# A larger ring of exp tiles, paid for by the ring of DVE tiles, with new assumed delays in a planned kernel

## The chip, the cores and the metric

One core of one Trainium2 chip. The metric is the device time of one launch in microseconds. Ratios are the mean time of one kernel's fast runs over the mean of the other's fast runs of the same rounds, so not quite the ratio of the medians that are quoted.

## The reference

Two independent branches on sequences of 2048 rows and 640 columns, side by side in the output: a diagonal state-space model, and attention with 32 heads of 20 columns over one shared key and value head.

```python
h = Lam_bar * h + Bu[t]                        # for each t
y = 2.0 * einsum("blp,dp->bld", hseq, Cmat).real + x * Dskip
...
scores = einsum("bhqd,bkd->bhqk", q, k) * (Dh ** -0.5)
p = softmax(scores, axis=-1)
o = einsum("bhqk,bkd->bhqd", p, v)             # then @ wo
return concatenate([a, b], axis=-1)
```

The attention decides the time: 32 heads of 2048 x 2048 scores are 2048 tiles of 128 x 512, and each element needs an exponential.

## The kernel before: the parts that matter

Before anything is built, Python plans the whole run: a discrete-event planner with assumed durations and assumed delays from engine to engine picks, for each engine, what it does next. Only the order that comes out is emitted, with the waits that the data need. The planner is run with 24 seeds, and the plan that it thinks ends first is taken.

```python
class Schedule:
    OUT = {"pe": 200.0, "act": 130.0, "dve": 110.0, "pool": 150.0, "dma": 60.0}   # end -> seen elsewhere, ns
...
    def planned(self):
        for seed in range(self.PLANS):            # 24
            ...                                   # keep the plan with the smallest end
```

ACT takes score tiles by two or three in one exp instruction. A *fill* is the PE step that writes the scores of the next exp (and perhaps a tile for DVE) into one of two three-bank slots:

```python
    def fill(self, op, i):
        n = min(self.cap[i], NTILE - self.tile_n)
        if n == 3 and self.want_own():
            own = self.take_d(used)               # third bank: a tile for DVE
        if own is not None:
            n = 2                                 # then ACT's exp has two tiles
        ...
        h = self.pr_take(n)                       # n slots of the exp ring (NPT = 24)
```

DVE tiles get an integer approximation of exp: one first step (reads PSUM), then three shifted copies made by DVE or POOL, so that one tile uses four slots of a second ring. It has `NDS = 20` slots, and `MORE = 21` further ones once the memory of the transposed input, the query weights and the query tiles is free (10, 6 and 5 slots; the change leaves it the first 10). A tile goes to DVE only if slots are free:

```python
    def want_own(self):
        ...
        return len(self.d_free()) > len(self.SHIFTS) - 1       # 4 shifts

    def can_d(self):
        ...
        if b > self.pv_b and len(self.d_free()) < len(self.SHIFTS) + self.due_copies():
            return False                          # a tile of the next block needs more free slots
```

*Fillers* are matmuls without use, meant to keep TensorE's clock up: before the attention and at its start (`warm_source`), and later, 256 columns wide, wherever the planner counts fewer than `KEEP = 3500` columns in 3 us (`keep_source`).

Of the kernel before, what the change touches and what calls it, by code (L numbers as in the profile page):

```python
# [42 lines left out]
class Schedule:  # L43
# [3 lines left out]


    ENGINES = ("pe", "act", "dve", "pool", "sp")
    OUT = {"pe": 200.0, "act": 130.0, "dve": 110.0, "pool": 150.0, "dma": 60.0}  # L50
    OWN = {"pe": 0.0, "act": 60.0, "dve": 115.0, "pool": 100.0}
    URGENT = 1.0

# [74 lines left out]
    def begin(self, op, eng):  # L128
        if op.hook is not None:
            op.hook(op)  # L130
        op.start = self.t
        if op.late:
            self.late_from = self.t + op.dur + self.PAUSE
        if eng == "pe":
            if op.mode != self.mode:
                op.dur += self.SWITCH
                self.mode = op.mode
            self.loads.append((self.t, op.load))
        if op.port:
            if eng == "pool" and self.port_last["dve"] is not None:  # L140
                op.after.append(self.port_last["dve"])
            self.port_free[eng] = self.t + op.dur + (self.LOCK if eng == "pool" else 0.0)
            self.port_last[eng] = op
            self.at(self.port_free[eng])
        if op.dma_key is not None:
            self.free[eng] = self.t + op.tail * len(op.fns)
            s = max(self.t + 1300.0, self.dma_free.get(eng, 0.0), self.pipe)
            self.dma_free[eng] = self.pipe = s + op.dur
            op.end = max(s + op.dur + 700.0, self.free[eng] + 1700.0) + op.land
        else:  # L150
            if op.table is not None and op.table != self.table:
                self.table = op.table
                op.dur += self.TABLE
            op.end = self.t + op.dur + op.tail
            self.free[eng] = self.t + op.dur - (self.EARLIER.get(eng, 0.0) if op.psum else 0.0)
        self.order.append(op)
        self.at(self.free[eng])
        for lag in (0.0, 60.0, 100.0, 110.0, 115.0, 130.0, 150.0, 200.0):
            self.at(op.end + lag)

    stay = staticmethod(lambda: True)
# [253 lines left out]
class Build:  # L415
# [3 lines left out]
    NOP = 7  # L419
    NRD = 3  # L420
    NDS = 20
    MORE = 21
    SHARE = 0.265

    SHIFTS = ((0, 0.2421875), (32, 0.201171875), (64, 0.169921875), (96, 0.142578125))
# [13 lines left out]
    def build(self):  # L439
        nc = self.nc  # L440
        with ExitStack() as o:
            self.banks = []
            self.slots = []
            sizes = list(self.CHUNKS) + [1] * (8 - sum(self.CHUNKS))
            self.psum = [o.enter_context(nc.psum_tensor(f"{'SC' if i < len(self.CHUNKS) else 'MB'}{i}", [128, 512 * n], FP32))
                         for i, n in enumerate(sizes)]
            self.alloc(o)
            base = nc.sbuf_bytes_remaining
            with ExitStack() as p1:
                self.alloc_early(p1)  # L450
                early = base - nc.sbuf_bytes_remaining
            with ExitStack() as p2:
                self.alloc_late(p2)
                late = base - nc.sbuf_bytes_remaining
                if late < early:
                    self.sb(p2, "pad", [128, (early - late) // 4 + 8], FP32)
                plan = self.planned()
                shares = {k: self.EARLY for k in self.LATE}
                shares.update({k: self.EARLY for k in ("pb0", "pb1", "lb", "qt")})
                shares.update({f"W{c}_0": self.EARLY + ["pb0", "pb1"] for c in range(NC)})  # L460
                shares.update({f"W{c}_1": self.EARLY + ["lb", "qt", "pc0", "pc1"] for c in range(NC)})
                shares.update({"pc0": ["lb"], "pc1": ["qt"]})
                shares.update({f"CB{c}": [f"xbT{i}_{k}" for i in range(2) for k in range(NC)] for c in range(NC)})
                shares.update({f"CT{tb}_{c}": [f"xn{tb}"] for tb in range(2) for c in range(NC)})
                shares.update({f"DR{self.NDS + i}": over for i, over in enumerate(self.dr_over)})
                shares["WOt"] = [f"BT{i}_{c}" for i in range(2) for c in range(NC)]
                shares.update({f"OPT{k}": [f"BA{i}_{c}" for i in range(2) for c in range(NC)] for k in self.EARLY_O})
                em = Emitter(nc, plan.s.order, [b.key for b in plan.banks], shares)
                em.plan()
                with nc.Block() as block:  # L470
                    em.emit(block)
# [36 lines left out]
    def alloc(self, o):  # L508
# [9 lines left out]
        for c in range(NC):  # L518
            for m in range(2):
                self.dr_at.append(2048 * c + 640 + 512 * m)  # L520
                self.dr_over.append([f"xbT{i}_{c}" for i in (1, 2, 3)])
        for m in range(6):
            self.dr_at.append(ends[0] + 512 * m)
            self.dr_over.append(["wqa", "wqb"])
        for m in range(NC):
            self.dr_at.append(ends[1] + 512 * m)
            self.dr_over.append([f"QP{m}"])
        self.xaT = sb(o, "xaT", [128, NC, 2, 512], BF16)
        self.BT = sb(o, "BT", [128, 2, NC, 640], BF16)
        self.BA = sb(o, "BA", [128, 2, NC, 640], BF16)  # L530
# [124 lines left out]
    def program(self):  # L655
        self.lay_banks()
        self.firsts, self.row_mm, self.stage_dma, self.buf_user, self.unit_due = [], {}, {}, {}, {}
        self.tile_n = 0
        self.rem = [[collections.deque(range(NKC)) for _ in range(4)] for _ in range(NQB * NGG)]
        self.act_b = 0  # L660
        self.free_banks = list(self.banks)
        self.vp_op, self.kt_op, self.vs_op = {}, {}, {}
        self.tasks = []
        self.evac_op, self.norm_op, self.part_op = {}, {}, {}
        self.q_op, self.qd_op, self.half_op, self.scat_op, self.rd_op, self.brow_op = {}, {}, {}, {}, {}, {}
        self.o_ops, self.y_ops, self.w_op, self.xa_op = {}, {}, {}, {}
        self.state_op = {}
        self.owner = [None] * self.NPT
        self.pr_at = 0
        self.waiting = []  # L670
        self.dhold = [Holder(i) for i in range(self.NDS)]
        self.d_open = []
        self.d_left = collections.defaultdict(int)
        self.d_count = 0
        self.d_per = collections.defaultdict(int)
        self.pvq = {b: [[], [], [], []] for b in range(NQB * NGG)}
        self.pv_filled = {b: 0 for b in range(NQB * NGG)}
        self.pv_b = 0
        self.pv_first = {}
        self.outs = 0  # L680
        self.s.stay = lambda: self.started
        self.constants()
        self.loads()
        self.kv_steps()
        self.ssm_scalars()
        self.background()
        self.s.spawn(self.attention())
        self.s.spawn(self.manager())
        self.s.spawn(self.late_loads())
        self.s.spawn(self.more())  # L690
        self.free_banks.remove(self.pvbank)
        self.s.sources["pe"].append(self.pv_source)
        self.s.sources["pe"].append(self.warm_source)
        self.s.sources["pe"].append(self.d_source)
        self.s.sources["pe"].append(self.keep_source)
        self.s.sources["dve"].append(self.copy_source)
        self.s.sources["act"].append(self.act_source)
        self.s.sources["pool"].append(self.pool_source)

    def warm_source(self):  # L700
# [3 lines left out]
        p = self  # L704
        if self.started:
            if self.s.recent(3000.0) > self.WARM:
# [1 line left out]
            fns = self.four(self.pvbank, [p.VZ[:]] * 4, p.KT[:, 0:512], True, True)  # L708
            return Op("pe", fns, self.mmt(512), prio=3.5, mode="C", load=512.0, reads=["VZ", "KT0"], writes=[self.pvbank.key],
                      deps=[self.c_op["VZ"], self.kt_op[0]])  # L710
        return Op("pe", [self.mm(self.pvbank.ap, p.PR[:, 0, 0:128], p.PR[:, 0, :], True, True)], 260.0, prio=9,
                  load=512.0, deps=[self.zero_op], reads=["PR0"], writes=[self.pvbank.key], hook=self.warm_last)

    WARM = 4500.0
    V_AT, BOUND_AT = (-88, -87), -99

# [467 lines left out]
    def fill(self, op, i):  # L1184
# [16 lines left out]
        ents = []  # L1201
        for x, m in enumerate(tiles):
            b, kc, j = self.score(op, m, t[:, 512 * x:512 * x + 512], banks[x])
            ents.append((b, kc, j, p.PR[:, h.index + x, :]))
        first = [] if own is None else [self.fill_d(op, own, banks[2])]
        if first:
            other = self.slot_last[1 - i][0]
# [6 lines left out]
        op.reads = sorted(set(op.reads))  # L1214
        op.dur = self.mmt(512, len(op.fns))
        op.load = 128.0 * len(op.fns)
        dst = p.PR[:, h.index:h.index + n, :]
        ex = self.act(lambda e: e.activation(dst, t[:, 0:512 * n], ACT.Exp, scale=1.0 / UNIT),  # L1218
                      0.8333 * 512 * n + 64, table="exp",
                      deps=[op], reads=[b.key for b in banks[:n]], writes=keys, prio=0.5,  # L1220
# [32 lines left out]
        return h  # L1253

    def pr_next(self, n):
        return self.pr_at if self.pr_at + n <= self.NPT else 0

    def tight(self):

# [171 lines left out]
    def more(self):  # L1431

        yield lambda: NQB - 1 in self.row_mm and self.s.done([self.row_mm[NQB - 1]]) \
            and all(self.s.done([self.qd_op[NQB - 1, i]]) for i in range(NC))
        self.dhold += [Holder(self.NDS + i) for i in range(self.MORE)]

    def d_free(self):

# [865 lines left out]
```

## Time and profile before

| | before |
|---|---|
| median of six runs | 745.13 us (744.28 to 746.13) |
| span of the profiled run | 743.5 us |
| first exp starts, last exp ends | 23.02, 734.42 us |
| exps: two tiles, three tiles | 475, 201 |
| tiles on ACT, on DVE | 1553, 495 |

Two quantities are used throughout. The **bare ACT time** is what the exps would take without any wait: 904 ns from the start of a two-tile exp to the next start, 1331 ns for a three-tile one, and the whole of the last one. **Late starts** are the sum, over all exps, of what their distance exceeds these numbers by. The start of the first exp, bare time, late starts and the tail after the last exp add up to the span: 23.0 + 697.2 + 14.2 + 9.1 = 743.5.

### The profile page before, as it was taken

The numbers are of one execution on the slowest core, as the hardware profiler recorded it, in microseconds if no ns is written. First come the engines' busy times: TensorE is split into PE (matmuls) and PEld (weight loads), VectorE is DVE, ScalarE is ACT, GpSimd is POOL, SyncE is SP. The second block draws the span as 40 slices with busy tenths as digits, with TensorE's granted clock in tenths as the row PEclk, the third lists the DMA queues.
The fourth block names the chain that finished last, engine by engine and source line by source line (L and its number), as shares of the span: only waits on it lengthen the run. The fifth ranks groups of instructions, "written<-read, shape, count | busy, mean of one in ns | idle before, by whom it ended". The sixth has DMA issues, their size and how long they took to land.

```text
span 743.5 us, 26647 instructions
## 1 busy us (share of the span) xinstructions
PE 711.7 (96%) x11323; PEld 255.9 (34%) x11323; DVE 665.3 (89%) x1367; ACT 722.9 (97%) x702; POOL 426.3 (57%) x448
## 2 busy tenths in 40 slices
PE   9999899998999999999999999989999999999997
PEld 3422222234443533332333333323333333332332
DVE  6888999989788798999898999998998998988995
ACT  5999999999999999999999999999999999999995
POOL 3766566430266558367476674566754835778460
PEclk9999999999999999999999999998999999999999
DMA  9414443364220100101100000110000011100101
GB/s 200 70 41 129 91 113 90 89 144 78 48 60 10 25 20 21 51 11 35 42 26 23 17 30 19 40 46 19 19 14 19 9 27 30 37 16 17 26 14 37
DMA packets 78089, 34.43 MB, mean 46 GB/s; under 512 B 58852, under 2 KB 77972, under 8 KB 77972
## 3 DMA queue, kind: packets, MB, share of 16 engines
q1 hardware_dynamic: 76352, 32.34, 18.3%
q8 instruction: 90, 1.47, 0.8%
q10 hardware_dynamic: 1620, 0.39, 0.3%
q14 instruction: 27, 0.22, 0.1%
HBM read 11.53 MB, written 9.75 MB: 29 GB/s over the span
## 4 chain that ended last, share of the span: by engine, by line
ACT 59%; PE 34%; DVE 6%; issue 1%; DVEq 0%
ACT PR L1218 59%; PE MB L637 12%; PE SC L637 11%; PE MB L633 10%; DVE BIG L652 2%; DVE prod L647 1%; DVE W L652 1%; DVE CT L647 1%; DVE CA L647 1%; DVE g L2046 0%; PE SC L633 0%; DVE pvsb L1580 0%; DVE CT L651 0%; DVE CA L651 0%; PE SC L935 0%
## 5 line engine op out<-in xcount | busy, mean ns | idle before, releaser
L1218 ACT ACTIVATE PR<-SC 128x1024 bf16<-128x1024 f32 (+1 forms) x676 | 708.6, 1252 | 3.3 <-PE SC L637 2.1
L647 POOL TENSOR_TENSOR BIG<-BIG,step 128x512 int32<-128x512 int32 x401 | 407.4, 1045 | 286.1 <-DVE BIG L652 163.1
L652 DVE TENSOR_SCALAR BIG<-SC 128x512 int16<-128x512 f32 x456 | 302.8, 684 | 38.5 <-PE SC L637 34.9
L637 PE MATMUL SC<-QT,KT 32*128 32x512 bf16 x2009 | 265.3, 386 | 23.0 <-ACT PR L1218 16.0
L637 PE MATMUL MB<-BIG,VS 128*32 128x512 bf16 x1980 | 248.5, 386 | 1.2 <-issue 0.6
L637 PE MATMUL MB<-PR,VP 128*32 128x512 bf16 x1553 | 217.4, 386 | 0.8 <-DVE pvsb L1580 0.6
L637 PEld LDWEIGHTS SC<-QT,KT 32*128 32x128 bf16 x2009 | 67.8, 91 | 258.2 <-ACT PR L1218 165.3
L652 DVE TENSOR_SCALAR BIG<-BIG 128x1024 int16<-128x1024 int16 (+1 forms) x356 | 129.0, 419 | 8.6 <-PE MB L637 7.0
L637 PEld LDWEIGHTS MB<-BIG,VS 128*32 128x32 bf16 x1980 | 62.6, 95 | 66.7 <-issue 44.1
L637 PEld LDWEIGHTS MB<-PR,VP 128*32 128x32 bf16 x1553 | 53.5, 94 | 54.6 <-issue 41.0
L633 PE MATMUL MB<-CT,W 128*32 128x320 bf16 (+2 forms) x1040 | 49.7, 301 | 0.2 <-DVE BIG L2006 0.2
L633 PE MATMUL MB<-xaT,BT 128*32 128x256 bf16 x800 | 34.5, 274 | 0.0
L633 PE MATMUL MB<-xaT,BA 128*32 128x256 bf16 x800 | 33.6, 274 | 0.1
L633 PE MATMUL MB<-CA,W 128*32 128x512 bf16 (+1 forms) x640 | 31.2, 301 | 0.1
L647 DVE TENSOR_TENSOR prod<-MB,tab 128x1024 bf16<-128x1024 f32 x20 | 24.3, 1215 | 3.7 <-PE MB L633 3.7
L652 DVE TENSOR_SCALAR BIG<-MB 128x512 int16<-128x512 f32 x39 | 26.5, 680 | 1.1 <-PE MB L637 0.7
L633 PEld LDWEIGHTS MB<-CT,W 128*32 128x32 bf16 x1040 | 21.4, 96 | 17.0 <-issue 7.9
L633 PE MATMUL MB<-WO,OP 128*32 128x128 bf16 (+1 forms) x576 | 26.5, 297 | 0.1
L1761 DVE CAST stg<-MB 128x512 bf16<-128x512 f32 x35 | 23.9, 683 | 2.6 <-PE MB L633 2.3
L633 PE MATMUL MB<-BIG 128*32 128x512 bf16 x340 | 25.6, 383 | 0.0
L2046 DVE TENSOR_TENSOR_SCAN g<-sc,hst,prod 128x256 bf16<-128x256 f32 x30 | 23.1, 776 | 0.0
L633 PEld LDWEIGHTS MB<-xaT,BA 128*32 128x32 bf16 x800 | 19.0, 96 | 9.0 <-issue 5.4
(167 smaller groups left out, 421.2 us busy)
## 6 DMA issues: line engine op xcount, KB each, us to landing
out_dram<-stg SPq DMA_DIRECT2D x31, 128.0 KB, 1.7
qd<-BIG SPq DMA_DIRECT2D x20, 128.0 KB, 1.8
QT<-qd SPq DMA_DIRECT2D x28, 80.0 KB
OP<-pvsb SPq DMA_DIRECT2D x105, 20.0 KB
rdP<-recs SPq DMA_DIRECT2D x105, 20.0 KB
W<-in_A_B_re_dram SPq DMA_DIRECT2D x10, 160.0 KB, 2.7
W<-in_A_B_im_dram SPq DMA_DIRECT2D x10, 160.0 KB, 2.7
lbd<-W SPq DMA_DIRECT2D x10, 160.0 KB, 2.0
```

The costliest lines, as they stand in the source:

```text
L633: r = e.matmul(out[32 * j:32 * j + 32], lhsT=lhsT[:, 32 * j:32 * j + 32], rhs=rhs, start=start, stop=stop, tile_position=(0, 32 * j), skip ...
L637: return lambda e: e.matmul(out, lhsT=lhsT, rhs=rhs, start=start, stop=stop, **kw)
L647: return lambda e: e.tensor_tensor(out, a, b, op)
L652: return lambda e: e.tensor_scalar(out, a, s1, s2, op0=op0, op1=op1)
L1218: ex = self.act(lambda e: e.activation(dst, t[:, 0:512 * n], ACT.Exp, scale=1.0 / UNIT), 0.8333 * 512 * n + 64, table="exp", deps=[op], re ...
L1761: ev = self.dve(lambda e: e.tensor_copy(st, bank.ap), 645, deps=[prev], reads=[bank.key], writes=[key], prio=self.EV, gate=(lambda: last.e ...
L2046: o = self.dve(lambda e, ri=ri, init=init: e.tensor_tensor_scan(p.g[:, u, ri, :], rdec, p.prod[:, 1, 0, ri, :], init, ALU.mult, ALU.add), ...
```

## The change

The intent: an exp must not wait for a slot of its ring, so the ring gets eleven more slots, taken from the DVE ring, which (on average) had many free. At the same time the planner's delays are set nearer to what a trace shows, and the fillers at the start are counted at the low clock.

```diff
-    OUT = {"pe": 200.0, "act": 130.0, "dve": 110.0, "pool": 150.0, "dma": 60.0}
+    OUT = {"pe": 215.0, "act": 225.0, "dve": 110.0, "pool": 150.0, "dma": 60.0}
...
-    MORE = 21
+    MORE = 10
...
-        for m in range(6):
-            self.dr_at.append(ends[0] + 512 * m)
-            self.dr_over.append(["wqa", "wqb"])
-        for m in range(NC):
-            self.dr_at.append(ends[1] + 512 * m)
-            self.dr_over.append([f"QP{m}"])
+        self.wide_at = [(self.NPT, 6, ends[0]), (self.NPT + 6, NC, ends[1])]
+        self.pr_over = [["wqa", "wqb"]] * 6 + [[f"QP{m}"] for m in range(NC)]
...
-        return Op("pe", [... p.PR[:, 0, :] ...], 260.0, prio=9,
+        return Op("pe", [... p.PR[:, 0, :] ...], self.COLD if self.s.t < self.WARMED else 240.0, prio=9,
...
+    COLD, WARMED = 450.0, 6000.0
...
     def pr_next(self, n):
-        return self.pr_at if self.pr_at + n <= self.NPT else 0
+        ends = [self.NPT] + ([at + k for at, k, _ in self.wide_at] if self.wide else [])
+        end = next((e for e in ends if e > self.pr_at), None)
+        ...                                       # goes round through 24, 6 and 5 slots
...
         self.dhold += [Holder(self.NDS + i) for i in range(self.MORE)]
+        self.wide = True
```

More of the change, by code (lines that the diff above doesn't have):

```diff
@@ L157, in begin @@
         self.at(self.free[eng])
-        for lag in (0.0, 60.0, 100.0, 110.0, 115.0, 130.0, 150.0, 200.0):
+        for lag in (0.0, 60.0, 100.0, 110.0, 115.0, 150.0, 215.0, 225.0):
             self.at(op.end + lag)
@@ L465, in build @@
                 shares.update({f"DR{self.NDS + i}": over for i, over in enumerate(self.dr_over)})
+                shares.update({f"PR{self.NPT + i}": over for i, over in enumerate(self.pr_over)})
                 shares["WOt"] = [f"BT{i}_{c}" for i in range(2) for c in range(NC)]
@@ L667, in program @@
         self.state_op = {}
-        self.owner = [None] * self.NPT
+        self.owner = [None] * (self.NPT + len(self.pr_over))
+        self.wide = False
         self.pr_at = 0
@@ L710, in warm_source @@
                       deps=[self.c_op["VZ"], self.kt_op[0]])
-        return Op("pe", [self.mm(self.pvbank.ap, p.PR[:, 0, 0:128], p.PR[:, 0, :], True, True)], 260.0, prio=9,
+        return Op("pe", [self.mm(self.pvbank.ap, p.PR[:, 0, 0:128], p.PR[:, 0, :], True, True)], self.COLD if self.s.t < self.WARMED else 240.0, prio=9,
                   load=512.0, deps=[self.zero_op], reads=["PR0"], writes=[self.pvbank.key], hook=self.warm_last)
+    COLD, WARMED = 450.0, 6000.0
     WARM = 4500.0
@@ L1203, in fill @@
             b, kc, j = self.score(op, m, t[:, 512 * x:512 * x + 512], banks[x])
-            ents.append((b, kc, j, p.PR[:, h.index + x, :]))
+            ents.append((b, kc, j, self.pr(h.index + x, 1)[:, 0, :]))
         first = [] if own is None else [self.fill_d(op, own, banks[2])]
@@ L1216, in fill @@
         op.load = 128.0 * len(op.fns)
-        dst = p.PR[:, h.index:h.index + n, :]
+        dst = self.pr(h.index, n)
         ex = self.act(lambda e: e.activation(dst, t[:, 0:512 * n], ACT.Exp, scale=1.0 / UNIT),
@@ L1255, in pr_next, with pr @@
     def pr_next(self, n):
-        return self.pr_at if self.pr_at + n <= self.NPT else 0
+        ends = [self.NPT] + ([at + k for at, k, _ in self.wide_at] if self.wide else [])
+        end = next((e for e in ends if e > self.pr_at), None)
+        if end is None:
+            return 0
+        if self.pr_at + n <= end:
+            return self.pr_at
+        return end if end < ends[-1] else 0
+    def pr(self, i, n):
+        for at, k, base in self.wide_at:
+            if at <= i < at + k:
+                lo = base + 512 * (i - at)
+                return self.BIG[:, lo:lo + 512 * n].rearrange("p (i n) -> p i n", n=512)
+        return self.PR[:, i:i + n, :]
     def tight(self):
```

## The prediction

> **What bounds the kernel now.** The kernel lays down, before it is built, one fixed order of instructions for each engine; a planner with assumed durations and assumed delays decides it, and the chip then follows it. 2048 score tiles (128x512) each need an exponential: most go to ACT in instructions of two or three tiles, the rest to DVE and POOL by an integer trick. I read the busy times first, then the chain.
>
> ```profile
> PE 711.7 (96%) x11323; PEld 255.9 (34%) x11323; DVE 665.3 (89%) x1367; ACT 722.9 (97%) x702; POOL 426.3 (57%) x448
> PEclk9999999999999999999999999998999999999999
> ACT 59%; PE 34%; DVE 6%; issue 1%; DVEq 0%
> ```
>
> ACT is busy 97% and holds 59% of the chain that ended last; PE's 96% needs checking, since its matmuls are pipelined. So I took the ACT groups by shape, and who waits for whom.
>
> ```profile
> L1218 ACT ACTIVATE PR<-SC 128x1024 bf16<-128x1024 f32 x475 | 447.9, 1112 | 2.0 <-PE SC L637 1.4
> L1218 ACT ACTIVATE PR<-SC 128x1536 bf16<-128x1536 f32 x201 | 277.9, 1585 | 1.3 <-PE SC L637 0.7 <-PE MB L637 0.4
> ...
> PEld SC L637 <- ACT PR L1218: 165.3, 410, 1.2
> PEld SC L637 <- DVE BIG L652: 60.1, 144, 0.9
> ACT PR L1218 <- PE SC L637: 2.1, 5, 0.6
> ```
>
> PE's score matmuls wait for ACT (410 times) and for DVE (144 times) to free a score bank; ACT shows only 3.3 us idle before its 676 exps. The timeline gives the real cost of one exp, from start to start:
>
> ```profile
> 23.02 5.61 ACT L1218 ACTIVATE PR<-SC 128x1024 bf16<-128x1024 f32 x6 [0.58 <-PE SC L637]
> ...
> 164.22 5.69 ACT L1218 ACTIVATE PR<-SC 128x1536 bf16<-128x1536 f32 x4
> ```
>
> Six two-tile exps in 5.61 us, the last of them some 1.1 long, give about 0.90 us each; four three-tile ones, 1.33. Over the whole trace the median distances are 904 and 1331 ns. First exp at 23.02, last one ends at 734.42, end of the span at 743.5. So the 711.4 us of exps are 474 x 0.904 + 201 x 1.331 = 696.0, plus 1.2 for the last, plus **14.2 us in which exps started late**. Most of that is not shown as idle: a start that is up to 0.2 us late hides under the tail of the exp before. It nearly all follows two-tile exps (13.8 us), and its pattern is PE work between two score fills that doesn't fit into 0.904 us:
>
> ```profile
> 322.80 0.39 PE L637 MATMUL SC<-QT,KT 32*128 32x512 bf16 x3
> 323.12 1.26 PE L633 MATMUL MB<-BIG,xaT 128*32 128x512 bf16 x20
> 324.32 0.39 PE L637 MATMUL SC<-QT,KT 32*128 32x512 bf16 x3
> ...
> 324.76 1.02 ACT L1218 ACTIVATE PR<-SC 128x1024 bf16<-128x1024 f32 x1 [0.29 <-PE SC L637]
> ```
>
> Twenty matmuls stand between two fills, and the exp at 324.76 starts 0.56 us late.
>
> **What the Trainium skill says.** "Perfetto Trace Analysis", Identifying the Most-Contended Engine: occupancy judges ACT, DVE and POOL, but matmul busy share doesn't judge TensorE. The trace agrees: PE at 96% still waits 165 us for ACT. The same page, DVE / Act Engine Instruction: an ACT record ends with the acknowledged write, and that is when the semaphore goes out, while the next instruction may begin earlier. The trace agrees: exps are 1112 ns long but 904 apart, so a waiting engine sees the end some 208 ns after ACT has moved on. The planner puts the end at 0.8333 x 1024 + 64 = 917 and adds 130: 1047, which is earlier than the 1112 measured even before the signal travels. 225 gives 1142, close to it. "ScalarE: Activation LUTs", Rules for kernel authors: about 0.83 ns per element; here (1331 - 904) / 512 = 0.834. "TensorE: Matmul & The Clock Gate", What's actually happening: an idle window of about 3.4 us halves the clock, a busy one restores it. The trace's clock record has one such loss, 502.46 to 509.29; the exps in it are late by 626, 181, 609 and 183 ns, 1.6 us of the 14.2.
>
> **The change, part by part.** All counts are from the instruction orders of the two builds.
> (1) *Exp ring 24 to 35 slots, DVE ring 41 to 30, once all queries are made.* The first exp that writes into the new slots is the 151st of 672. Was the old ring a limit? ACT waits for PE in two sizes only (2.1 us for scores, 0.4 for the matmuls that free ring slots), so on the chip hardly. The planner calls the ring tight at 186 of 914 groups of value matmuls before, 123 of 908 after; groups with fewer than four members are 60 and 69. PE gains little: 24 value matmuls fewer (3533 to 3509), 24 quarter-size keep-warm ones more. The DVE ring had on average 19 slots free, and 11 after: not starved.
> (2) *Share of tiles.* DVE takes 495 tiles before and 487 after, so ACT takes 1553 and 1561. In instructions: 475 two-tile and 201 three-tile become 455 and 217. Bare ACT time after: 455 x 0.904 + 216 x 1.331 + 1.6 = 700.4, before 696.0 + 1.2 = 697.2. **Cost: +3.2 us, all on the path that sets the end.** DVE in return loses 8 first steps of 0.68 us and POOL 10 double steps of 1.05: off the path.
> (3) *Delays: ACT 130 to 225, PE 200 to 215.* Emits no instruction, only another order. I cut the PE order at the score fills and added the work between them (a 512-column matmul of a quarter array counts 512 / 2.4 / 4 = 53 ns). Before, 54 two-tile intervals hold 650 ns or more, late by 122 ns on average, 6.6 us together; those with less are late by 17 on average. After there are 45 such intervals. With the mean lateness of each size class of before, the changed order gives 13.0 us: -1.1. I take another 1.3 off because an order made with a truer ACT delay should meet fewer surprises, and because DVE is a little less loaded, and 0.8 for an even chance that the clock loss doesn't return. **Late starts about 11.0 us: -3.2.** The last two are judgement.
> (4) *Fillers at the cold clock.* Twenty warm-up matmuls stand before the first transposes, and they delay them:
>
> ```profile
> 4.02 1.89 PE L637 MATMUL MB<-PR 128*128 128x512 bf16 x4
> ...
> 7.47 2.12 PE L637 MATMUL MB<-PR 128*128 128x512 bf16 x9
> 9.44 0.78 PE L637 MATMUL SC<-ident,CT 128*128 128x128 bf16 x11
> ```
>
> The first block of x landed at 6.06, but the transposes start at 9.44, behind nine fillers. A filler takes about 0.43 us cold and 0.23 warm; twelve remain, six of them in the last run. If the clock rises at 7.5 as before, the transposes can begin some 0.9 us earlier, and part of that reaches the first exp, as the later input columns land until 14.97 anyway: -0.6. If fewer fillers leave PE too idle and the clock rises a window (3.4 us) later, the head loses about 1 us. Two to one: **-0.1, rounded.**
> The tail (9.1 us after the last exp) has the same operations in nearly the same order: 0.
> Sum: 745.9 + 3.2 - 3.2 - 0.1 = 745.8; I say **745.5 us**.
>
> **Rivals.** *A: the ring was the hidden limit.* Then the larger one makes the late starts fall to about 7 us: 741 to 742. For it: 186 tight decisions, which pull value matmuls ahead of other work. Against: the ACT waits on ring slots are 0.4 us. *B: ACT's share alone decides.* DVE takes fewer tiles, the late starts stay at 14: 749. For it: each tile moved to ACT costs 0.44 to 0.45 us directly. *C: the clock decides.* Fewer fillers delay the warm-up, or further clock losses of 1.6 us each come: 749 to 751. For it: one loss happened before; against: 380 keep-warm matmuls stand for 356.
>
> **Range and chances.** The floor, with no late start at all, is 700.4 + 32.1 of head and tail + the 2.4 between span and stated time = 734.9, so over 2% faster (731) is out of reach short of a mistake in these terms. Slower by over 2% (761) would need the late starts to double. Rivals A and C set the ends: **741 to 750**, with 0.02 for faster, 0.96 within 2%, 0.02 slower.
>
> **What would show it right or wrong.** Step 2: the ACT groups of 455 and 217 with unchanged distances. Step 3: late starts summed over all exps; 9 to 13 is right, under 8 means A, over 14 B. Step 4: the start of the first transposes (8.5 right, 9.4 or later wrong), and the first exp before 23.0. I am wrong if exps wait for freed ring slots, if DVE waits for free slots, or if the clock is lost more than twice.

## The result, and the profile after

748.86 us median of six runs (748.04 to 750.60) against 745.13: ratio 1.0052, interval 1.0035 to 1.0068. Slower by half a per cent, within the predicted range, but on the other side of the predicted gain of next to nothing.

The page of the kernel after: busy times, granted clock in 40 slices, and the chain that ended last.

```profile
PE 711.7 (95%) x11320; PEld 256.0 (34%) x11320; DVE 657.7 (88%) x1360; ACT 726.0 (97%) x698; POOL 416.7 (56%) x438
PEclk9899999999999999999999999999999999999999
...
ACT 66%; PE 30%; SPq 1%; DVE 1%; DMA 1%; issue 0%; DVEq 0%
```

ACT is busy 3.1 us longer, DVE 7.6 and POOL 9.6 us shorter: work has gone from DVE and POOL to ACT, which is the engine that sets the time. The ACT groups by shape (count | busy us, mean ns | idle before):

```profile
L1217 ACT ACTIVATE PR<-SC 128x1024 bf16<-128x1024 f32 x347 | 333.8, 1120 | 4.0 <-PE SC L634 2.4 <-PE MB L634 1.1
L1217 ACT ACTIVATE PR<-SC 128x1536 bf16<-128x1536 f32 x171 | 240.9, 1638 | 0.0
L1217 ACT ACTIVATE BIG<-SC 128x1024 bf16<-128x1024 f32 x108 | 107.5, 1115 | 0.5 <-PE SC L634 0.4
L1217 ACT ACTIVATE BIG<-SC 128x1536 bf16<-128x1536 f32 x46 | 67.3, 1608 | 0.2 <-PE MB L634 0.2
```

347 + 108 = 455 exps of two tiles, 171 + 46 = 217 of three: 1561 tiles against 1553. Exps that write into the old query memory (BIG) are as fast as the others: in both groups the median distance from start to start is 904 ns for two tiles and 1330 ns for three, as the stretches of exps below show (4 x 0.904 + 1.1 is 4.7 us, 5 x 0.904 + 1.1 is 5.6, 2 x 1.33 + 1.6 is 4.3; the last exp of each counts with its whole length).

```profile
290.08 4.75 ACT L1217 ACTIVATE BIG<-SC 128x1024 bf16<-128x1024 f32 x5
...
329.52 5.61 ACT L1217 ACTIVATE PR<-SC 128x1024 bf16<-128x1024 f32 x6 [0.20 <-PE SC L634]
...
729.45 4.22 ACT L1217 ACTIVATE BIG<-SC 128x1536 bf16<-128x1536 f32 x3
...
733.44 4.27 ACT L1217 ACTIVATE PR<-SC 128x1536 bf16<-128x1536 f32 x3
```

The waits:

```profile
PEld SC L634 <- ACT PR L1217: 126.7, 308, 0.9
...
PEld SC L634 <- DVE BIG L649: 50.6, 117, 0.9
...
PEld SC L634 <- ACT BIG L1217: 36.2, 89, 0.9
```

PE waits for ACT as long as before (126.7 + 36.2 = 162.9 against 165.3 us). The span taken apart by the start times in the timelines of the two profiled runs:

| us | before | after | difference |
|---|---|---|---|
| first exp starts | 23.02 | 22.43 | -0.6 |
| bare ACT time | 697.2 | 700.4 | +3.2 |
| late starts, clock whole | 12.5 | 12.2 | -0.3 |
| late starts within 1 us of a clock loss | 1.7 | 2.7 | +1.0 |
| tail | 9.1 | 9.1 | 0.0 |
| span | 743.5 | 746.8 | +3.3 |

So in this pair of profiled runs nearly all of it is the eight tiles and their shapes. That is an account of where the time went; whether undoing a part gives the time back is asked below. Two lines of the PE timeline show the shorter head, with six fillers ahead of the transposes in place of nine, started two microseconds earlier:

```profile
5.34 2.74 PE L634 MATMUL MB<-PR 128*128 128x512 bf16 x6
7.87 1.15 PE L634 MATMUL SC<-ident,CT 128*128 128x128 bf16 x16
```

The transposes start at 7.87 instead of 9.44, but the first exp gains only 0.6 of the 1.6 us: the last two blocks of transposed input landed at 15.47 and 16.59 us in this run, 1.6 later than in the run before, and PE waits for one of them (0.17 us). The rest of what was lost on the way isn't taken apart.

Where the clock is lost shows in the busy times by stretch (length, then busy us and instructions of PE, PEld, DVE, ACT, POOL, then the granted clock):

```profile
25.10:28.50 3.40, 2.69 (x37) 1.87 (x41) 3.30 (x16) 3.40 (x5) 3.02 (x7) 1.00 0.50 113
28.50:35.40 6.90, 6.90 (x54) 1.34 (x52) 3.11 (x9) 5.09 (x6) 4.10 (x10) 0.51 0.09 21
```

From 28.5 to 35.4 us TensorE has half its clock, and ACT is busy for 5.09 of 6.90 us. The exps there start late one after the other:

```profile
31.29 1.02 ACT L1217 ACTIVATE PR<-SC 128x1024 bf16<-128x1024 f32 x1 [0.30 <-PE SC L634]
33.24 1.02 ACT L1217 ACTIVATE PR<-SC 128x1024 bf16<-128x1024 f32 x1 [0.93 <-PE MB L634]
34.74 1.02 ACT L1217 ACTIVATE PR<-SC 128x1024 bf16<-128x1024 f32 x1 [0.48 <-PE SC L634]
```

### The profile page after: what moved, and what is told of

Same layout as the page of the kernel before. It is cut to its first block, busy times and chain, and to the rows that moved or that the text cites. A ratio compares the mean times of both kernels' runs of the same rounds, so it can differ in the third digit from the quotient of the medians.

```text
span 746.8 us, 26570 instructions
## 1 busy us (share of the span) xinstructions
PE 711.7 (95%) x11320; PEld 256.0 (34%) x11320; DVE 657.7 (88%) x1360; ACT 726.0 (97%) x698; POOL 416.7 (56%) x438
## 4 chain that ended last, share of the span: by engine, by line
ACT 66%; PE 30%; SPq 1%; DVE 1%; DMA 1%; issue 0%; DVEq 0%
ACT PR L1217 51%; ACT BIG L1217 15%; PE MB L630 10%; PE SC L634 9%; PE MB L634 9%; SPq L619 1%; PE SC L630 1%; DMA BIG<-in_B_x_dram 1%; DVE prod L644 0%; DVE BIG L649 0%; PE SC L934 0%; SPq L615 0%; DVE PR L644 0%; DVEq L471 0%; DVE BIG L2019 0%
## 5 line engine op out<-in xcount | busy, mean ns | idle before, releaser
L644 POOL TENSOR_TENSOR BIG<-BIG,step 128x512 int32<-128x512 int32 x391 | 397.8, 1045 | 299.0 <-DVE BIG L649 145.8
L1217 ACT ACTIVATE PR<-SC 128x1024 bf16<-128x1024 f32 (+1 forms) x518 | 558.1, 1291 | 4.0 <-PE SC L634 2.4
L649 DVE TENSOR_SCALAR BIG<-SC 128x512 int16<-128x512 f32 x435 | 290.3, 685 | 42.0 <-PE SC L634 37.7
L634 PE MATMUL MB<-BIG,VS 128*32 128x512 bf16 x1948 | 218.8, 384 | 0.8 <-DVE BIG L649 0.7
L1217 ACT ACTIVATE BIG<-SC 128x1024 bf16<-128x1024 f32 (+1 forms) x154 | 170.5, 1262 | 0.7 <-PE SC L634 0.4
L634 PE MATMUL MB<-PR,VP 128*32 128x512 bf16 x1207 | 160.2, 386 | 0.1
L634 PEld LDWEIGHTS SC<-QT,KT 32*128 32x128 bf16 x1996 | 68.3, 91 | 259.3 <-ACT PR L1217 126.7
L634 PEld LDWEIGHTS MB<-BIG,VS 128*32 128x32 bf16 x1948 | 55.0, 95 | 62.1 <-issue 38.8
L634 PEld LDWEIGHTS MB<-PR,VP 128*32 128x32 bf16 x1207 | 40.2, 95 | 42.1 <-issue 30.7
L634 PE MATMUL MB<-BIG,VP 128*32 128x512 bf16 x354 | 53.6, 385 | 0.0
L649 DVE TENSOR_SCALAR BIG<-MB 128x512 int16<-128x512 f32 x52 | 35.4, 680 | 4.3 <-PE MB L634 4.3
```

The source lines that it names most:

```text
L634: return lambda e: e.matmul(out, lhsT=lhsT, rhs=rhs, start=start, stop=stop, **kw)
L644: return lambda e: e.tensor_tensor(out, a, b, op)
L649: return lambda e: e.tensor_scalar(out, a, s1, s2, op0=op0, op1=op1)
L1217: ex = self.act(lambda e: e.activation(dst, t[:, 0:512 * n], ACT.Exp, scale=1.0 / UNIT), 0.8333 * 512 * n + 64, table="exp", deps=[op], re ...
```

## The experiments

**Theory.** ACT's share of the tiles sets the time; the smaller DVE ring makes the planner refuse DVE tiles; the new delays gain nothing; clock losses of TensorE come on top. **Rivals:** the larger exp ring or the truer delays do remove late starts; the new slots are themselves slow; the difference is the luck of one plan among 24.

First a count without a chip. The number of DVE tiles in each of the 24 plans, for each combination of parts:

```
                                    DVE tiles, mean of 24 (range)   chosen plan
before                              492.7 (489-496)                 495
delays alone                        495.2 (493-498)                 497
fillers alone                       490.5 (487-495)                 495
ring alone                          484.3 (479-489)                 487
DVE ring smaller, exp ring as is    487.2 (483-490)                 488
all three (the change)              484.0 (481-487)                 487
```

And why, once the queries are made, a fill that could have had a DVE tile got none (in the chosen plan; in the second row in plan 6, that of the kernel before):

```
                                    given  no free slots  next block needs slots  state-space work overdue
before                              376    0              54                      102
DVE ring smaller, exp ring as is    366    13             89                      63
ring alone                          365    20             71                      75
the change                          360    24             63                      71
```

So the smaller DVE ring costs 5.5 tiles on average, the ring part as a whole 8.4: the ranges of 24 plans hardly overlap with that of before, so the draw of one plan doesn't make that. Why the larger exp ring takes a further 2.9 tiles wasn't looked into. The mean of free slots (19 before, 11 after) hid that they run out in bursts.

All chip runs, with the kernel before in the same rounds. *Late* is of the profiled run: with the clock whole + at clock losses. *Clock* is the mean granted clock over all fast runs.

| run | DVE tiles | exps 2 / 3 | bare us | late us | clock | median us | ratio (95%) |
|---|---|---|---|---|---|---|---|
| before | 495 | 475 / 201 | 697.2 | 12.5 + 1.7 | 0.9956 | 744.7 to 745.1 | 1 |
| after | 487 | 455 / 217 | 700.4 | 12.2 + 2.7 | 0.9938 | 748.86 | 1.0052 (1.0035-1.0068) |
| e1_delays | 497 | 474 / 201 | 696.2 | 14.4 + 4.6 | 0.9930 | 748.61 | 1.0051 (1.0039-1.0063) |
| e2_ring | 487 | 464 / 211 | 700.6 | 11.8 + 0 | 0.9990 | 746.31 | 1.0021 (1.0008-1.0034) |
| e3_fillers | 495 | 475 / 201 | 697.2 | 14.0 + 0.9 | 0.9928 | 747.74 | 1.0036 (1.0021-1.0050) |
| e4_less_dve | 488 | 463 / 211 | 699.7 | 12.0 + 0 | 0.9996 | 745.75 | 1.0008 (0.9996-1.0020) |
| e5_no_ring | 492 | 463 / 210 | 698.4 | 14.2 + 6.7 | 0.9918 | 750.80 | 1.0077 (1.0053-1.0101) |
| e6_no_delays | 482 | 447 / 224 | 702.5 | 10.5 + 2.6 | 0.9953 | 748.93 | 1.0053 (1.0032-1.0074) |
| e7_no_fillers | 484 | 452 / 220 | 701.6 | 13.0 + 2.4 | 0.9910 | 752.67 | 1.0108 (1.0076-1.0139) |
| e8_before_keep | 491 | 472 / 204 | 698.4 | 12.7 + 2.6 | 0.9958 | 747.19 | 1.0031 (0.9999-1.0063) |
| e9_after_keep | 487 | 453 / 218 | 699.9 | 12.8 + 1.4 | 0.9962 | 748.21 | 1.0047 (1.0023-1.0072) |
| e10_early_work | 487 | 455 / 217 | 700.4 | 13.4 + 0 | 0.9955 | 751.32 | 1.0083 (1.0067-1.0099) |
| e11_before_plan10 | 489 | 466 / 209 | 699.7 | 11.9 + 3.4 | 0.9947 | 748.25 | 1.0046 (1.0033-1.0059) |
| e12_after_plan11 | 485 | 451 / 220 | 700.7 | 10.7 + 2.6 | 0.9947 | 748.56 | 1.0047 (1.0029-1.0065) |

(The bare times in the expectations below leave out the tail of the last exp, so they are 0.2 to 0.3 us smaller.)

### e1_delays: the delays alone

```diff
-    OUT = {"pe": 200.0, "act": 130.0, ...}
+    OUT = {"pe": 215.0, "act": 225.0, ...}
```

> Part 3 alone: the delays (ACT 130 to 225, PE 200 to 215), ring and fillers as before. The built order gives DVE 497 tiles (before 495); exps 474 two-tile and 201 three-tile, bare ACT time 696.0 us against 696.9. Theory (the bare ACT time, set by DVE's share, decides; late starts stay near 12.5 plus what a clock loss costs): about 0.9 us faster, ratio 0.998 to 1.000. Rival A (truer delays remove late starts, as the prediction took): late starts near 10, 3 to 4 us faster, ratio 0.995. Rival B (the delays do the harm): slower, ratio 1.003 or more.

Ratio 1.0051: rival B, against my theory and against the prediction. DVE takes two tiles *more* and the bare ACT time falls, yet the run is slower. The profiled run is an expensive one (748.3 us, 4.8 more than before's): bare -1.0, late starts with a whole clock +1.9, four clock losses in place of one +3.0, head and tail +0.9. Here is the first loss after 90 us and the stretch before it:

```profile
94.88:98.30 3.42, 2.08 (x19) 0.52 (x13) 3.42 (x7) 3.42 (x5) 1.59 (x2) 1.00 0.71 175
98.30:101.70 3.40, 3.37 (x31) 0.76 (x31) 3.00 (x6) 2.96 (x4) 3.40 (x5) 0.50 0.48 144
```

Only 19 matmuls in 3.4 us, none of the gaps between them longer than 0.6 us, and then half the clock for 3.4 us. What the delay does to late starts can be read from four pairs of kernels that differ in nothing else: late starts with a whole clock go from 12.5 to 14.4 (nothing else changed), 14.0 to 14.2 (with the fillers), 11.8 to 13.0 (with the ring) and 10.5 to 12.2 (with both). Up each time, by 1.9, 0.2, 1.2 and 1.7 us, but with one profile each, and another plan of the same kernel moves this figure nearly as much (e11 by -0.6 against before, e12 by -1.5 against the change). So the new delays bring no gain that shows; that they do harm by themselves isn't settled.

### e2_ring and e4_less_dve: both rings, and the DVE ring alone

```diff
-    MORE = 21                    # e4: this alone
+    MORE = 10
                                  # e2: and the exp ring takes the 11 slots, as in the change
```

> Part 1 alone: exp ring 24 to 35, DVE ring 41 to 30; delays and fillers as before. The built order gives DVE 487 tiles, exps 464 and 211, bare ACT time 700.3 us. Theory: slower by 3.4 us, ratio 1.0045. Rival (the larger exp ring removes late starts, which pays for the tiles): late starts down to 9 or 10, ratio about 1.000.

> Half of part 1: the DVE ring shrinks from 41 to 30, and the 11 slots are left unused; the exp ring stays at 24. DVE 488 tiles, exps 463 and 211, bare ACT time 699.4 us. Theory (the lost DVE slots are the cost, by way of refused DVE tiles): slower by 2.5 us, ratio 1.0035, close to the ring change as a whole. Rival (the eleven exp slots in the old query memory are the cost, by waits or by slower writes there): ratio 1.000, and only the ring run slower.

Both have the bare time that the tiles dictate (+3.4 and +2.5 us), and both show fewer late starts than before. The ACT groups of e4_less_dve:

```profile
L1218 ACT ACTIVATE PR<-SC 128x1024 bf16<-128x1024 f32 x463 | 436.1, 1122 | 1.4 <-PE SC L637 0.9 <-PE MB L637 0.3
L1218 ACT ACTIVATE PR<-SC 128x1536 bf16<-128x1536 f32 x211 | 292.5, 1585 | 1.0 <-PE SC L637 0.6 <-PE MB L637 0.4
```

But the ratios are only 1.0021 and 1.0008, less than the tiles cost and less than my theory's 1.0045 and 1.0035; by their ratios alone both lie nearer to the rivals' 1.000, though e2's late starts (11.8) didn't fall to the 9 or 10 of its rival. The difference that the record shows is the clock: **neither lost it at all**. Their mean clock is 0.999 and above in all runs, where the kernel before has 0.988 to 1.000. That this is what hid the cost of the tiles rests on the estimate under "Time and clock together". The same early stretch as above, in e2_ring:

```profile
28.50:35.40 6.90, 6.90 (x99) 2.42 (x99) 4.99 (x13) 6.90 (x8) 4.82 (x11) 1.00 0.15 40
```

ACT is busy for all of the 6.90 us. The larger exp ring on its own (e2 against e4) bought no time: 1.0021 against 1.0008, with one DVE tile fewer. The eleven slots lie idle in e4 without harm, so with the old delays the exp ring was no limit.

### e3_fillers: the count of fillers alone

```diff
-    ... 260.0, prio=9,
+    ... self.COLD if self.s.t < self.WARMED else 240.0, prio=9,
```

> Part 4 alone: fillers counted at 450 ns until 6 us. DVE 495 tiles, exps 475 and 201, bare ACT time as before, 696.9. Theory: the first exp 0.6 us earlier, else as before; a clock loss soon after the head as in the changed kernel (2.7 us there) if the fillers cause it. So ratio 0.999 without that loss, 1.003 with it.

The first exp starts at 22.52 (-0.5), the tiles are unchanged, and still 1.0036. The plan is another one (seed 21 in place of 6), with 1.5 us more late starts, and its clock was lower (0.989 to 0.997). The fastest of its runs, 745.46, is the one with the highest clock. The loss in the profiled run was at 503.7 us, not early, so the fillers alone don't explain the early one.

### e5_no_ring, e6_no_delays, e7_no_fillers: the change with one part undone

> The changed kernel with its ring part undone (exp ring 24, DVE ring 41; new delays and fillers stay). DVE 492 tiles, exps 463 and 210, bare ACT time 698.1 us against 700.1 with the ring. If the ring part is what costs, this gains 2 us on the changed kernel and lands near 746.5 (ratio to the kernel before 1.002). If the delays are what costs, as their run alone said (1.0051), it stays at 748 or more (ratio 1.004 to 1.006), with late starts outside the clock losses at 14 or more and a mean clock of 0.993.

> The changed kernel with the old delays (ACT 130, PE 200); ring and fillers stay. DVE 482 tiles, exps 447 and 224, bare ACT time 702.2 us, 2.1 more than the changed kernel. If the bare ACT time decides alone: 750, ratio 1.007. If the new delays cost some 2 us in late starts and some clock, which going back gives back: 747 to 748, ratio 1.003 to 1.004.

> The changed kernel with the old fillers (260 ns each); ring and delays stay. DVE 484 tiles, exps 452 and 220, bare ACT time 701.4 us, 1.3 more than the changed kernel. If the parts add up, 748.5 to 750 (ratio 1.004 to 1.007), with late starts outside clock losses near 12. If the filler count is what brings the early clock loss at 25 to 35 us, that loss is gone, mean clock 0.998, and the time 747.

All three are slower than the kernel before, and none is clearly better than the change. Without the ring part the change is not faster, as my theory had it, but at 1.0077, beyond both branches, on the side of the one that blames the delays: the new delays without the ring have three clock losses in the profile (6.7 us) and 14.2 us of late starts, although DVE has five tiles more than in the change and the bare ACT time is 2.0 us less. So undoing the ring part doesn't give the time back, and the tiles' cost is shown by the account of the profiles and not by this run. Without the new delays: 1.0053, as the change, with 2.1 us more bare time and 1.7 us fewer late starts (three of its six runs have 2.7 to 2.9 us between span and launch time, where nearly all others have 1.7 to 2.0; by spans its ratio is 1.0046). Without the new fillers: 1.0108, with a clock down to 0.985 in two runs, and the early clock loss came all the same, at 26.9 us (in e1_delays, which has the old fillers too, at 26.6), so the new filler count isn't needed for it. The parts don't add up: 0.51 + 0.21 + 0.36 per cent alone make 1.08, together they cost 0.52. Every part makes the planner draw a new plan, which may be why; that isn't shown.

### e8_before_keep and e9_after_keep: more keep-warm matmuls

```diff
-    KEEP = 3500.0
+    KEEP = 4200.0
```

> The kernel before with the threshold for keep-warm matmuls raised from 3500 to 4200 columns in 3 us, nothing else. DVE 491 tiles, exps 472 and 204, bare ACT time 698.2 us, 1.3 more. If low activity of TensorE causes the clock losses: mean clock 0.998 or more in every run, and the loss of about 1.7 us per event gone, so 744 to 745.5, with a smaller spread of the times than the 2.4 us of before. If the losses have another cause: clock 0.992 to 0.998 as before, 746.5.

> The changed kernel with the same threshold raised from 3500 to 4200. DVE 487 tiles, exps 453 and 218, bare ACT time 699.7 us, 0.4 less. If the clock losses cost the changed kernel 2 to 3 us and come of low TensorE activity: mean clock 0.998 or more, 745 to 746.5, ratio 1.000 to 1.002. If not: 748.5, clock 0.993 to 0.995.

A miss. The clock is still lost: in e8 at 503.7 us, where the kernel before loses it, in e9 at 30.2. Both kernels have runs at 0.998 or above and runs at 0.991 or below. The threshold counts columns that the *planner* thinks flow in 3 us, and places fillers only where the planner thinks PE idle; that it therefore misses stretches in which the chip's PE waits or streams little is argued from the code, not shown.

### e10_early_work: idle columns where the changed kernel loses the clock

```diff
+    def idle(self, bank):
+        return [self.mm(bank.tensor[32*j:32*j+32, bank.off+256:bank.off+512], p.VZ[:], p.KT[:, 0:256],
+                        True, True, tile_position=(0, 32*j), skip_group_check=True) for j in range(4)]
...
-            prev = self.pe([lambda e, blk=blk: e.matmul(bank.cols(blk, blk + 1), ...)], 250.0, ...
+            prev = self.pe(self.idle(bank) + [lambda e, blk=blk: e.matmul(bank.cols(blk, blk + 1), ...)], 250.0, ...
```

(and the same behind each value projection of the last two row blocks; the results of the idle matmuls are never read)

> The changed kernel with 52 idle quarter-array matmuls of 256 columns on zero weights (13 groups of 4), hung onto the small matmuls between 20 and 31 us. The order on every engine stays the same otherwise. If too little array work between 25 and 28.5 us is what loses the clock there: no loss at 25 to 35 us, mean clock up from 0.994 to 0.997 or more, and 1.5 to 2.7 us faster than the changed kernel, so 746.3 to 747.3, ratio 1.0015 to 1.003. If the loss has another cause: clock and time as in the changed kernel, 749, ratio 1.005.

Half of it came. In the profiled run the early loss is gone, and late starts fall from 14.9 to 13.4 us:

```profile
PEclk9999999999999999999999999999999999999999
```

Two of six runs have 0.999, which no run of the changed kernel reached (0.993 to 0.995); the other four have 0.993 to 0.994, and no profile tells where they lost it. The time got worse: four groups of idle matmuls landed ahead of the first score matmuls, and an input block landed 0.7 us later in this run (17.28 us against 16.59), so that the first exp starts at 24.08 instead of 22.43. The run supports low array work as the cause of the early loss; it doesn't settle it (late starts with a whole clock went up, from 12.2 to 13.4), and it is no improvement: 1.0083, where 1.0015 to 1.003 was expected.

### e11_before_plan10 and e12_after_plan11: another plan, the same kernel

```diff
-        for seed in range(self.PLANS):
+        for seed in (10,):        # e12: (11,), in the changed kernel
```

> The kernel before with another of its own 24 plans (number 10 in place of 6); no part of the change. DVE 489 tiles, exps 466 and 209, bare ACT time 699.4 us, 2.5 more. If DVE's share of tiles sets the time whatever lowers it: 1 to 2.5 us slower at the same clock (fewer two-tile exps take a little off the late starts), ratio 1.0015 to 1.0035. If it is the rings themselves and not the share: ratio 1.000.

> The changed kernel with the plan that its planner ranked second, by 0.04 us (number 11 in place of 1). DVE 485 tiles, exps 451 and 220, bare ACT time 700.5 us, 0.4 more. If the changed kernel's loss is a property of the change: within 1 us of it, ratio 1.004 to 1.007. If the chosen plan was an unlucky draw: outside of that by 1.5 us or more, through the clock or the late starts.

e11 has nothing of the change in it, only a plan with six tiles fewer on DVE, and it is as slow as the change: 1.0046, above the 1.0035 expected at the most. (Of the 24 plans it has the fewest DVE tiles, 489.) Bare +2.5 us as its tiles dictate, late starts with a whole clock -0.6, head and tail -0.3, and two clock losses that cost 3.4 us where before has 1.7:

```profile
L1218 ACT ACTIVATE PR<-SC 128x1024 bf16<-128x1024 f32 x466 | 440.4, 1124 | 3.6 <-PE SC L637 3.1
L1218 ACT ACTIVATE PR<-SC 128x1536 bf16<-128x1536 f32 x209 | 289.5, 1595 | 1.3 <-PE SC L637 0.7 <-PE MB L637 0.4
```

e12, the changed kernel's second-best plan, is at 1.0047, beside the change's 1.0052. So the change's loss isn't peculiar to the one plan that was chosen; two plans of 24 were run.

### Time and clock together

Over all fast runs, each kernel around its own mean, the time falls by 0.45 us for each 0.001 of mean granted clock (a fit; 0.6 us remain as scatter). Read off at a whole clock, an estimate, before is at 743.1 (33 runs of the experiment rounds) and the change at 746.2 (its own six): 3.1 us apart, which agrees within the scatter with the bare ACT time of the moved tiles. The mean clock (0.9938 against 0.9956) gives another 0.8. That is the 3.9 us between the mean times (749.01 against 745.08). On the same scale e11 is at 745.9, e2 at 746.0, e4 at 745.5: in these three, fewer DVE tiles cost 2.4 to 2.9 us. But the tiles are not the only thing that costs so much: e1_delays with two *more* DVE tiles is at 745.7, e5_no_ring with only three fewer at 747.2, e8_before_keep with four fewer at 745.7. These have the new delays or more keep-warm matmuls.

## Why the prediction was right or wrong

The range held (741 to 750; measured 748.9), the middle was 3.4 us low. Its base mixed two runs: 745.9 was a median, while the profiled run took 745.3, so from span to stated time it is 1.8 us and not 2.4; this made the middle 0.6 higher.

**Step 1, the rings: half right.** The old exp ring was indeed no limit on the chip (e2 against e4). But "19 free on average, 11 after: not starved" was a wrong inference. In the planner's count the slots run out in bursts: 24 refusals for want of any slot against none before, and 63 against 54 at the border of two blocks. It did no harm to the number, since the tiles were counted from the built order.

**Step 2, the share of tiles: right.** +3.2 us of bare ACT time predicted, +3.2 measured, with unchanged distances of 904 and 1331 ns.

**Step 3, the late starts: this step failed.** I took them from 14.2 down to 11.0; they are 14.9 (12.2 with a whole clock, 2.7 at the clock loss), over the 14 that the prediction itself had named as rival B's sign. Of the three terms, the one from the PE order (-1.1) has the right sign for the crowded intervals only: with a whole clock the 45 of them are late by 4.1 us, the 54 of before by 6.6 (that sum's clock losses lie outside them). The intervals with little PE work between fills, which I had taken as constant, got worse: from 5.7 us over 414 to 7.9 over 403. The second term, that a truer ACT delay means fewer surprises (-1.3), isn't borne out: in all four pairs late starts rose with the new delays, though by little more than another plan moves them (by up to 1.9 us against up to 1.5). Why isn't shown; that a later believed ACT end lets the planner put more PE work ahead of a fill is only argued. The third, an even chance that the clock loss goes away (-0.8), went the other way: it came back at another place and larger (2.7 us against 1.7). The prediction had also taken the loss for one after an idle window; the 3.4 us ahead of it, 499.05 to 502.46, hold 24 matmuls with no idle gap over 0.6 us.

**Step 4, fillers: too small, right sign.** -0.6 at the first exp in place of -0.1. The transposes gained more than the 0.9 us I gave them (1.6), and 1.0 of it was lost again on the way to the first exp; input that landed 1.6 us later is the one cause seen. The warm-up came at 8.0 us, 0.5 later than before, not a window later.

**Rivals.** B (ACT's share alone, 749) was nearest. By the account above that is in part luck: it leaves out the clock, which took 1.0 us more, and the head, which gave 0.6 back. C holds for the runs' scatter and for part of the difference. A is refuted: with a whole clock the late starts are 12.2 us, not 7.

**What stays open:** whether the new delays make more late starts by themselves, and why; what exactly decides a clock loss; and why the ring part saves time beside the new delays (1.0077 without it, 1.0052 with it, intervals that overlap), when it costs beside the old ones. No run beat the kernel before.

## What to carry to other kernels

Where a planner fixes the order, read from the built order what the engine that sets the time will have to do: the count of its instructions by shape, times the measured distance, gave the direct cost of the change to a tenth of a microsecond before it ran. A buffer with many free slots on average may still be the one that is short; count the refusals, not the mean. And judge a half-per-cent change against other plans of the same kernel and at the same granted clock, for a mere change of seed, to the plan with the fewest DVE tiles, moved this one as much as the whole change did.

## What the Trainium skill lacked or had wrong

- "TensorE: Matmul & The Clock Gate", Why this matters for your kernels: it asks for no PE-idle gaps over about 3 us to avoid a loss of clock in mid-kernel; the page's section on psum-queue depth-cycling adds that frequent micro-idles between groups of matmuls can do it too, but gives no measure for them. Here the clock was lost 18 times in 11 profiled runs with no idle gap over 1.0 us before it. What those 18 have in common is that columns streamed through the array for only 20 to 39% of the 3.4 us ahead of the loss (median of all such windows: 66 to 69%; an estimate that counts 54 ns for a matmul of 512 columns on a quarter of the array, as the 20 in 1.26 us at 323.12 us show). Windows as low passed without a loss too, one of 25% at 587.8 us in the kernel before and one of 30% at 49.7 us in e3_fillers, so it is no rule. A busy PE row in the trace doesn't show it: 2.69 of 3.40 us before the changed kernel's loss.
- The same page, What's actually happening: the window of about 3.4 us agrees; the losses last 3.4 or 6.8 us, one 10.2. What a loss costs a kernel that TensorE doesn't bound is not there: here 1.7 to 2.7 us for one of 6.8 (before, after, e6, e8, e12).
- "ScalarE: Activation LUTs", What ACT_TABLE_LOAD costs: back-to-back ACTIVATEs are said to overlap by about 93 ns. Here two-tile exps are 1112 ns long in the mean and 904 apart, an overlap of about 208.
- No page says how much the mean granted clock varies from run to run of one kernel, one core in use: 0.988 to 1.000 for the kernel before, with 742.9 to 748.3 us.
